# Attention and mixture of experts on one core: high and low parts of q and k made once and placed by transfers, token rows in pairs of d's, 256-column copies on VectorE

## The chip, the cores and the metric

The kernel runs on one core of a Trainium2 chip. The metric is the device time of one execution in microseconds (us). Three runs of the kernel before took 944.52, 946.16 and 946.60 us; the median, 946.16 us, is the time to which the change is compared.

## The reference

Attention with a decay bias over 64 heads (8 batches of 8), then a top-1 mixture of experts over the 4608 tokens, all in float32:

```python
scores = scale * np.matmul(q, k.transpose(0, 1, 3, 2))          # 8 x 8 x 576 x 576, head size 64
bias = -(cum[:, :, :, None] - cum[:, :, None, :])               # cum: running sum of max(s, 0)
scores = np.where(causal, -1e9, scores + np.minimum(bias, 0.0))
attn = softmax(scores)                                          # with 1e-9 added to the sum
x = (attn @ v) -> (B * S, H * D)                                # 4608 x 512
e_idx = argmax(x @ w_gate + modality_bias[modality_id])         # one of 8 experts a token
out[mask] = gate_w[mask, None] * (relu(x[mask] @ w1[e]) @ w2[e])
```

## The kernel before

**Stages.** The program first does attention for 32 pairs: a pair is one head of two batches (a = 0, 1), and eight pairs (the eight heads) make a group, which is 1152 finished tokens. After each group a routing step (`Route.group`) reads the tokens' gate values, finds each token's expert and slot, and nine indirect transfers issued by GpSimd (POOL, line 502) scatter the token rows into lists in HBM. After the attention the experts run over the lists (lines 657 to 886); their part of the program is not changed but for the order of the words in a token row.

**One pair.** A score is made in four steps. PE multiplies q by k twice into a PSUM tile `sp`: high parts (line 216: `QH` by `KA`, whose upper 64 rows are k's low part) and low parts with the bias rows (line 217: `QL` by `KB`). DVE adds the mask, copies the tile to `pe` in SBUF and finds the row's extreme (line 219). ACT takes the exponential (line 238). So it goes for nine tiles of a pair, in the order `ORDER`; the ninth, the rest of both batches, is `pep` (lines 230 to 238). Then `trans` turns each tile on PE (lines 248, 257) and copies it from PSUM into `PT`: on ACT (line 251), but for the numbers in `PTDVE`, which go to DVE (line 263). `tail` multiplies `V` by `PT` (lines 274, 279, into `o0` and `om`), copies the outcome to `oT` (ACT lines 283, 284; DVE line 287), multiplies by `pw` in two halves (lines 293, 296, into `ox`), and DVE scales and writes token rows `x` (lines 299, 301). `o0` and both halves share one PSUM buffer, `ox`.

**Operands.** q and k come from HBM in rows doubled on the host (`rawq`, `rawk`, 576 KB each a pair, line 152). `prep` rounds them to the matmul's format for the high parts and subtracts for the low ones: on POOL (lines 174, 192, 194), but for half of `QL`, which is on DVE (line 188) and reads what POOL has written. There are two sets of `QH`, `QL`, `KA`, `KB`; pair p+1's set is written while pair p runs. The bias rows of `KB` and `QL` come by transfers from HBM (lines 170, 171).

**The order.** The source interleaves the nine scores of a pair with the turning of tiles three steps behind (`LAG`), the tail of the pair before, the preparation of the next and the routing. The recording layer then sets one order for each engine from its own reckoning of when operands will be there. On the chip each engine works through its list in that order: an instruction whose operands are late holds everything behind it. SP issues the transfers in the same way.

Of the kernel before, what the change touches and what calls it, by code (L numbers as in the profile page):

```python
# [7 lines left out]
F32 = mybir.dt.float32  # L8
# [9 lines left out]
P = 128  # L18
KW = 576
XW = 72  # L20
# [7 lines left out]
PTDVE = (8,)  # L28


class Attn:
# [3 lines left out]
    def __init__(self, ctx, tc, qkv, s, ident, consts):  # L35
# [16 lines left out]
        self.mk = c.tile([P, 800], F32, name="mk")  # L52
        self.hold = [None]
        with tc.tile_pool(name="cst", bufs=1, side="right") as t1:
            sr = t1.tile([64, KW], F32, name="sr")
            nc.sync.dma_start(sr, s)
            raw = self.load_qk(0)
# [11 lines left out]
            self.raw = {0: raw}  # L69
            for _ in self.prep(0):  # L70
                pass
# [76 lines left out]
    def load_qk(self, pi):  # L148
        nc = self.nc
        raw = [self.ld.tile([P, 2, KW], F32, name="rawq"), self.ld.tile([P, 2, KW], F32, name="rawk")]  # L150
        for u in range(2):
            nc.sync.dma_start(raw[u], self.qkv[pi, :, 2 * KW * u:2 * KW * u + 2 * KW].rearrange("p (a k) -> p a k", a=2))
        return raw

    def load_v(self, pi):
        V = self.ld.tile([P, 2, 5, 64], F32, name="V", bufs=3)
        self.nc.sync.dma_start(V, self.qkv[pi, :, 4 * KW:].rearrange("p (a j d) -> p a j d", a=2, j=5))
        return V

    def load(self, pi):  # L160
        self.raw[pi] = self.load_qk(pi)
        self.V[pi] = self.load_v(pi)

    def prep(self, pi):
        nc = self.nc
        rq, rk = self.raw.pop(pi)
        QH, QL, KA, KB = (t[pi % 2] for t in (self.QH, self.QL, self.KA, self.KB))
        QHf, KAf = QH.bitcast(F32), KA.bitcast(F32)
        if pi:
            nc.sync.dma_start(KB.bitcast(F32)[64:74], self.ekd.rearrange("(a p) r k -> p r a k", a=2)[pi])  # L170
            nc.sync.dma_start(QL.bitcast(F32)[74:76, :, :KW], self.eqd.rearrange("(a p) r k -> p r a k", a=2)[pi])

        def high(o, i, e=None):
            (e or nc.gpsimd).tensor_scalar(o, i, 1.0, 1.0, ALU.mult, ALU.mult)  # L174

        lo, up = slice(0, 64), slice(64, P)
        for a in range(2):
            if pi:
                high(QH[:, a, :KW], rq[:, a])
            else:  # L180
                nc.scalar.copy(QH[:, a, :KW], rq[:, a])
        yield
        for a in range(2):
            high(KA[:, a], rk[:, a], nc.vector if pi == 0 and a == 0 else None)
        yield
        for a in range(2):
            if a == 0:
                nc.vector.tensor_tensor(QL[lo, a, :KW], rq[lo, a], QHf[lo, a, :KW], ALU.subtract)
            high(KB[lo, a], rk[lo, a], nc.vector if pi == 0 and a == 0 else None)
            yield  # L190
        for a in range(2):
            i = (nc.vector if pi == 0 and a == 0 else nc.gpsimd).tensor_tensor(KA[up, a], rk[up, a], KAf[up, a], ALU.subtract)  # L192
            yield
        (nc.vector if pi == 0 else nc.gpsimd).tensor_tensor(QL[lo, 1, :KW], rq[lo, 1], QHf[lo, 1, :KW], ALU.subtract)
        yield
# [7 lines left out]
    def score(self, st, i):  # L203
# [34 lines left out]
        nc.scalar.activation(t[:, :n], t[:, :n], AF.Exp, bias=m, scale=-1.0, accum_out=st["sums"][:, i:i + 1])  # L238
# [26 lines left out]
    def tail(self, st):  # L265
# [15 lines left out]
        nc.vector.tensor_scalar(rs, st["sums"], 1.0e-9, None, ALU.add)  # L281
# [7 lines left out]
        for g in range(2):  # L289
# [7 lines left out]
            src = xo[:, :4 * XW].rearrange("p (c a d) -> p a c d", c=2, a=2)  # L297
            rv = rs[:, 0:8].rearrange("p (a c) -> p a c", a=2)[:, :, 2 * g:2 * g + 2].unsqueeze(3).broadcast_to([P, 2, 2, XW])
            nc.vector.tensor_tensor(x[g][:, :, :, h].rearrange("p (a c) d -> p a c d", a=2), src, rv, ALU.mult)
            if g == 1:  # L300
                nc.vector.tensor_scalar(x[2][:, 0, :, h], xo[:, 4 * XW:5 * XW], rs[:, 8:9], None, ALU.mult)
            yield

    def run(self, npair, newx, done, setup):

        bg = []
        self.load(1)
# [669 lines left out]
```

## Time and profile before

| | us |
|---|---|
| median of three runs | 946.16 |
| profiled execution, its own time | 941.79 |
| its span, first to last instruction | 940.1 |
| busy in the span: PE / DVE / POOL / ACT | 860.9 / 633.8 / 576.1 / 527.5 |
| attention: first score, last write of a token row | 16.0, 465.3 |
| mean granted clock of PE, of full speed | 0.981 |

A profile of one execution stands behind these: each engine's instructions in time, what ended each wait, and the clock that PE was granted. Busy time is summed over stages with different limits, so the stage that the change touches is read by itself: the attention, about 16 to 465 us. A row of the grouped view gives line, engine, operation, tile, size, how often, then busy us, mean ns of one, the engine's idle us just before them and what ended most of it. A row of the timeline gives the start, the length, and in brackets the idle time before it and its releaser. A row of the stage table gives for each engine busy us and, behind x, its instructions, then the granted clock, the share of the DMA engines' time in use, and GB/s.

### The profile page before, as it was taken

The numbers are of one execution on the slowest core, as the hardware profiler recorded it, in microseconds if no ns is written. First come the engines' busy times: TensorE is split into PE (matmuls) and PEld (weight loads), VectorE is DVE, ScalarE is ACT, GpSimd is POOL, SyncE is SP. The second block draws the span as 40 slices with busy tenths as digits, with TensorE's granted clock in tenths as the row PEclk, the third lists the DMA queues.
The fourth block names the chain that finished last, engine by engine and source line by source line (L and its number), as shares of the span: only waits on it lengthen the run. The fifth ranks groups of instructions, "written<-read, shape, count | busy, mean of one in ns | idle before, by whom it ended". The sixth has DMA issues, their size and how long they took to land. (4 is left out here: it accounts for less than half of the span.)

```text
span 940.1 us, 16721 instructions
## 1 busy us (share of the span) xinstructions
PE 860.9 (92%) x5584; PEld 714.7 (76%) x5584; DVE 633.8 (67%) x1485; ACT 527.5 (56%) x1209; POOL 576.1 (61%) x478
## 2 busy tenths in 40 slices
PE   0799999799989998899988989999999999999984
PEld 0577777577667777677777979999999999999862
DVE  7477777577856778777556966566665566566771
ACT  3577776577656775587644525445544454454551
POOL 9576667666786766885064725556655465564760
PEclk9999999899999999999999999999999999999998
DMA  5743334533363335550577757666666666665940
GB/s 149 205 121 135 134 135 133 181 132 113 121 213 118 104 120 171 187 179 18 189 244 263 280 190 290 238 231 223 247 227 220 225 225 228 225 230 224 325 157 3
DMA packets 67564, 172.79 MB, mean 184 GB/s; under 512 B 12087, under 2 KB 12087, under 8 KB 67412
## 3 DMA queue, kind: packets, MB, share of 16 engines
q1 hardware_dynamic: 61620, 151.64, 47.1%
q0 software_dynamic: 5856, 20.06, 5.4%
q8 instruction: 45, 0.74, 0.3%
q14 instruction: 43, 0.35, 0.1%
HBM read 144.95 MB, written 26.80 MB: 183 GB/s over the span
## 5 line engine op out<-in xcount | busy, mean ns | idle before, releaser
L238 ACT ACTIVATE pe<-pe,mx 128x512 f32<-128x512 f32 (+3 forms) x256 | 143.8, 563 | 54.1 <-DVE mx L219 50.7
L279 PE MATMUL om<-PT,V 128*64 128x448 f32 (+3 forms) x640 | 124.9, 424 | 10.7 <-DVE PT L263 10.5
L791 ACT ACTIVATE hT<-hp 128x512 fp32r<-128x512 f32 x72 | 42.8, 595 | 156.9 <-PE hp L789 156.9
L251 ACT COPY PT<-pt 128x512 f32<-128x512 f32 (+3 forms) x256 | 106.7, 421 | 36.1 <-PE pt L248 28.9
L248 PE MATMUL pt<-ident,pe 128*128 128x128 f32 x640 | 121.9, 288 | 4.0 <-DVE PT L263 3.3
L219 DVE CUSTOM_DVE_ANT_0 pe<-sp,mk 128x512 f32<-128x512 f32 (+3 forms) x256 | 114.7, 478 | 12.9 <-PE sp L217 7.3
L775 POOL DMA_INDIRECT out<-ys,oi x36 | 37.3, 1037 | 133.5 <-DVE ys L774 50.5
L216 PE MATMUL sp<-KA,QH 128*128 128x256 f32 (+2 forms) x256 | 97.0, 386 | 20.1 <-DVE KA L192 16.0
L248 PEld LDWEIGHTS pt<-ident,pe 128*128 128x128 f32 x640 | 79.2, 146 | 40.5 <-issue 14.9
L174 POOL TENSOR_SCALAR QH<-rawq 128x576 fp32r<-128x576 f32 x62 | 47.0, 761 | 88.7 <-issue 80.9
L192 POOL TENSOR_TENSOR KA<-rawk,KA 64x576 fp32r<-64x576 f32 x63 | 95.9, 1541 | 2.6
L217 PE MATMUL sp<-KB,QL 76*128 76x256 f32 (+2 forms) x256 | 86.4, 343 | 7.3 <-DMA QL<-oh 7.3
L789 PE MATMUL hp<-xT,wcb 128*128 128x256 f32 x648 | 90.2, 283 | 1.6 <-DVE hT L792 1.6
L279 PEld LDWEIGHTS om<-PT,V 128*64 128x64 f32 x640 | 60.7, 136 | 40.6 <-DVE PT L263 14.9
L789 PEld LDWEIGHTS hp<-xT,wcb 128*128 128x128 f32 x648 | 83.6, 189 | 2.5 <-DVE hT L792 1.9
L792 DVE SCALAR_TENSOR_TENSOR hT<-hp,hT 128x512 fp32r<-128x512 f32 x72 | 49.2, 684 | 52.9 <-ACT hT L791 52.9
L789 PE MATMUL hp<-xT,wcc 128*128 128x256 f32 x528 | 76.4, 285 | 8.3 <-DVE hT L792 3.2
L768 PE MATMUL y<-wcb,hT 128*128 128x512 f32 x336 | 81.1, 398 | 0.0
L789 PE MATMUL hp<-xT,wca 128*128 128x256 f32 x552 | 78.1, 284 | 0.4 <-ACT xT L754 0.3
L789 PEld LDWEIGHTS hp<-xT,wcc 128*128 128x128 f32 x528 | 69.9, 194 | 9.3 <-DVE hT L792 3.4
L768 PEld LDWEIGHTS y<-wcb,hT 128*128 128x128 f32 x336 | 62.8, 188 | 14.8
L789 PEld LDWEIGHTS hp<-xT,wca 128*128 128x128 f32 x552 | 71.7, 190 | 1.3 <-ACT xT L754 0.5
(270 smaller groups left out, 1987.7 us busy)
## 6 DMA issues: line engine op xcount, KB each, us to landing
wrbw<-in_w SPq DMA_DIRECT2D x104, 512.0 KB
wraw<-in_w SPq DMA_DIRECT2D x56, 512.0 KB
rawq<-in_qkv SPq DMA_DIRECT2D x32, 576.0 KB
rawk<-in_qkv SPq DMA_DIRECT2D x32, 576.0 KB
xg<-lists SPq DMA_DIRECT2D x18, 576.0 KB
V<-in_qkv SPq DMA_DIRECT2D x32, 320.0 KB
lists<-z SPq DMA_DIRECT2D x8, 576.0 KB
ekd<-ek SPq DMA_DIRECT2D x1, 1440.0 KB
```

Of the source, the lines that this page charges most:

```text
L174: (e or nc.gpsimd).tensor_scalar(o, i, 1.0, 1.0, ALU.mult, ALU.mult)
L192: i = (nc.vector if pi == 0 and a == 0 else nc.gpsimd).tensor_tensor(KA[up, a], rk[up, a], KAf[up, a], ALU.subtract)
L216: nc.tensor.matmul(sp[:, :nn], QH[:, q0:q0 + P], KA[:, ab, :nn], start=True, stop=False)
L217: nc.tensor.matmul(sp[:, :nn], QL[:EXT, q0:q0 + P], KB[:EXT, ab, :nn], start=False, stop=True)
L219: ins = nc.vector.tensor_tensor_reduce(out=t[:, :n], in0=sp[:, :n], in1=self.mk[:, 512 - n:512], scale=-0.125, scalar=3.0e38, op0=ALU.add, ...
L238: nc.scalar.activation(t[:, :n], t[:, :n], AF.Exp, bias=m, scale=-1.0, accum_out=st["sums"][:, i:i + 1])
L248: nc.tensor.transpose(out=pt[:, P * j:P * j + P], in_=pe[:, P * j:P * j + P], identity=self.ident)
L251: cp(w[:, :, v:v + P], pt[:, :P * (c + 1)].rearrange("p (j q) -> p j q", q=P))
L279: nc.tensor.matmul(om[r, q0 - P:], V[:, ab, j, :], PT[ab][:, PTS * j + q0 if j < 4 else PTW - 64:PTS * j + KW if j < 4 else PTW], start=j ...
L768: self.last[0] = nc.tensor.matmul(y[u], hT[:, a, f, P * u:P * u + P], W[4 + f // 2][:, c, 512 * (f % 2):512 * (f % 2) + 512], start=f == 0 ...
L789: nc.tensor.matmul(hp[:, u], W[k][:, a, f:f + P], xT[:, c, k], start=k == 0 and i == 0, stop=k == 3 and i == 2)
L792: nc.vector.scalar_tensor_tensor(hT[:, 1, 2 * m:2 * m + 2], hp, 0.0, hs.bitcast(F32), ALU.max, ALU.subtract)
```

## The change

The host no longer doubles the rows: a pair's q (rows 0 to 63) and k (rows 64 to 127) come in one load `R` of 576 KB. `split` makes the high part `H` and the low part `L` of both at once, on POOL alone: two roundings and two subtractions of 128x576. `place` copies them into `QH`, `QL`, `KA` and `KB` by six transfers from SBUF to SBUF of 64 rows each (288 KB), and adds the two transfers of bias rows. `H` and `L` have one buffer each: the next `split` waits until the transfers have read them. `split` works two pairs ahead, `place` one pair ahead. Pair 0 is prepared as before, by `prep0`, from four loads of 64 rows.

Token rows hold d's in pairs (d pair, head, 2) where they held (d, head), so `x` is written in runs of two words; loads of `w1` and the reads of gate, token number and gate values follow. The sums of a pair are stored in the order in which `x` needs them. `PTDVE` takes tiles 1 and 5, the 128x256 copies, to DVE. The small sum in line 281 adds a tile of 1e-9 instead of a constant.

```diff
-PTDVE = (8,)
+PTDVE = (1, 5, 8)
...
+    def split(self, pi):
+        nc = self.nc
+        R = self.R.pop(pi)
+        H, L = (self.ld.tile([P, 2, KW], F32R, name=n, bufs=1) for n in ("H", "L"))
+        self.S[pi] = H, L
+        for a in range(2):
+            nc.gpsimd.tensor_scalar(H[:, a], R[:, a], 1.0, 1.0, ALU.mult, ALU.mult)
+            yield
+            nc.gpsimd.tensor_tensor(L[:, a], R[:, a], H[:, a].bitcast(F32), ALU.subtract)
+            yield
+
+    def place(self, pi):
+        nc = self.nc
+        H, L = (t.bitcast(F32) for t in self.S.pop(pi))
+        QH, QL, KA, KB = (t[pi % 2].bitcast(F32) for t in (self.QH, self.QL, self.KA, self.KB))
+        lo, up = slice(0, 64), slice(64, P)
+        nc.sync.dma_start(QH[lo, :, :KW], H[lo])
+        nc.sync.dma_start(QH[up, :, :KW], H[lo])
+        nc.sync.dma_start(KA[lo], H[up])
+        nc.sync.dma_start(KA[up], L[up])
+        nc.sync.dma_start(QL[lo, :, :KW], L[lo])
+        nc.sync.dma_start(KB[lo], H[up])
+        nc.sync.dma_start(KB[64:74], self.ekd.rearrange("(a p) r k -> p r a k", a=2)[pi])
+        nc.sync.dma_start(QL[74:76, :, :KW], self.eqd.rearrange("(a p) r k -> p r a k", a=2)[pi])
...
-        nc.scalar.activation(t[:, :n], t[:, :n], AF.Exp, bias=m, scale=-1.0, accum_out=st["sums"][:, i:i + 1])
+        o = 2 * (i % 4) + i // 4 if i < 8 else 8
+        nc.scalar.activation(t[:, :n], t[:, :n], AF.Exp, bias=m, scale=-1.0, accum_out=st["sums"][:, o:o + 1])
...
-        nc.vector.tensor_scalar(rs, st["sums"], 1.0e-9, None, ALU.add)
+        nc.vector.tensor_tensor(rs, st["sums"], self.eps, ALU.add)
...
-            src = xo[:, :4 * XW].rearrange("p (c a d) -> p a c d", c=2, a=2)
-            rv = rs[:, 0:8].rearrange("p (a c) -> p a c", a=2)[:, :, 2 * g:2 * g + 2].unsqueeze(3).broadcast_to([P, 2, 2, XW])
-            nc.vector.tensor_tensor(x[g][:, :, :, h].rearrange("p (a c) d -> p a c d", a=2), src, rv, ALU.mult)
+            src = xo[:, :4 * XW].rearrange("p (t d) -> p t d", t=4)
+            rv = rs[:, 4 * g:4 * g + 4].unsqueeze(2).broadcast_to([P, 4, XW])
+            nc.vector.tensor_tensor(x[g][:, :, :, h], src.rearrange("p t (d r) -> p t d r", r=2), rv.rearrange("p t (d r) -> p t d r", r=2), ALU.mult)
...
     def run(self, npair, newx, done, setup):
-        self.load(1)
+        self.load_r(1)
+        self.V[1] = self.load_v(1)
+        self.load_r(2)
+        for _ in self.split(1):
+            pass
...
-                    prepg = self.prep(pi + 1) if pi + 1 < npair else None
+                    if pi + 1 < npair:
+                        self.place(pi + 1)
+                    prepg = self.split(pi + 2) if pi + 2 < npair else None
                 self.score(sts[pi], i)
...
-                if k % 9 == 7 and pi + 2 < npair:
-                    self.load(pi + 2)
+                if k % 9 == 7:
+                    if pi + 3 < npair:
+                        self.load_r(pi + 3)
+                    if pi + 2 < npair:
+                        self.V[pi + 2] = self.load_v(pi + 2)
...
-    out = np.zeros((32, 128, 4 * KW + 640), np.float32)
+    out = np.zeros((32, 128, 2 * KW + 640), np.float32)
```

The source lines move by about 20 (line 216 of before is line 236 of the change, 219 is 239, 279 is 300, 299 is 320), and the recording layer sets another order, not only for the moved work.

On PE, before, from the last product of a pair (tile `sp_2211`) to the first product of `V` with its `PT`. The next pair reads the other set (`KA0`, `QH0`, `KB0`, `QL0`):

```order
L217 MATMUL sp_2211<-KB1_105,QL1_101 128x256
L216 MATMUL sp_2224<-KA0_102,QH0_98 128x512
L217 MATMUL sp_2224<-KB0_104,QL0_100 128x512
L216 MATMUL sp_2239<-KA0_102,QH0_98 128x512
L248 MATMUL pt_2216<-ident_61,pe_2156 128x128 x3
L217 MATMUL sp_2239<-KB0_104,QL0_100 128x512
L248 MATMUL pt_2233<-ident_61,pe_2175 128x128 x2
L216 MATMUL sp_2250<-KA0_102,QH0_98 128x384
L248 MATMUL pt_2246<-ident_61,pe_2187 128x128
L217 MATMUL sp_2250<-KB0_104,QL0_100 128x384
L216 MATMUL sp_2261<-KA0_102,QH0_98 128x256
L217 MATMUL sp_2261<-KB0_104,QL0_100 128x256
```

Four tiles of the next pair are finished here, both products, ahead of the products with `V` and of the tail. The same place in the changed kernel, the end of a pair's products with `V` and its tail, up to the next pair's tiles `sp_2078` and `sp_2092`; their first products (line 236) were made four rows above the first row shown:

```order
L300 MATMUL om_2119<-PT0_106,V_1679 64x448
L300 MATMUL om_2119<-PT2_108,V_1679 64x320
L300 MATMUL om_2119<-PT0_106,V_1679 64x320
L300 MATMUL om_2119<-PT2_108,V_1679 64x192
L300 MATMUL om_2119<-PT0_106,V_1679 64x192
L300 MATMUL om_2119<-PT2_108,V_1679 64x64
L300 MATMUL om_2119<-PT0_106,V_1679 64x64
L314 MATMUL ox_2160<-pw_111,oT0_109 128x144 x2
L314 MATMUL ox_2176<-pw_111,oT0_109 128x144 x2
L317 MATMUL ox_2176<-pw_111,oT0_109 128x72 x2
L237 MATMUL sp_2078<-KB1_105,QL1_101 128x512
L237 MATMUL sp_2092<-KB1_105,QL1_101 128x512
```

The second products of the next pair's first four tiles now stand behind the whole tail of the pair before. So it is listed at the end of pair 1 and of every pair from 4 to 30 (pairs are counted from 0), 28 times.

On DVE, before, the stretch that ends with the tail's first write of token rows (`x`); the masks are the next pair's:

```order
L219 ISA pe,mx<-sp,mk 128x384
L219 ISA mx 128x1
L219 ISA pe,mx<-sp,mk 128x256
L219 ISA mx 128x1
L281 TENSOR_SCALAR rs<-sums 128x9
L233 ISA pep,mx<-sp,mk 128x288
L233 ISA mx 128x1
L282 RECIPROCAL rs<-rs 128x9
L233 ISA pep,mx<-sp,mk,mx 128x288
L233 ISA mx 128x1
L287 COPY oT_109<-om 64x64 x2
L299 TENSOR_TENSOR x<-ox,rs 128x288
```

Five of the next pair's nine tiles are masked ahead of the first write. The same place in the changed kernel:

```order
L302 TENSOR_TENSOR rs<-sums,eps 128x9
L303 RECIPROCAL rs<-rs 128x9
L272 COPY PT_106<-pt 128x2x128
L308 COPY oT_110<-om 64x64 x2
L320 TENSOR_TENSOR x<-ox,rs 128x144x2 x2
L322 TENSOR_SCALAR xq<-ox,rs 128x36x2
L239 ISA pe,mx<-sp,mk 128x512
L239 ISA mx 128x1
L239 ISA pe,mx<-sp,mk 128x512
L239 ISA mx 128x1
L239 ISA pe,mx<-sp,mk 128x384
L239 ISA mx 128x1
```

The next pair's first mask comes behind both writes of `x` and that of `xq`. ACT's list follows: it has no exponential of the next pair ahead of the copies to `oT` (lines 304, 305).

The routing of a finished group moves too. Before, its DVE instructions stand singly between masks; in the changed kernel nine of them stand in one piece behind the last write of the group's last pair (`xq`), ahead of the next pair's first mask:

```order
L488 TENSOR_REDUCE lg<-x 128x32
L488 TENSOR_REDUCE lg<-xq 128x8
L490 TENSOR_TENSOR lg<-lg,mbs 128x72
L492 TENSOR_REDUCE rmx<-lg 128x9
L493 TENSOR_TENSOR lg<-lg,rmx 128x72
L497 SCALAR_TENSOR_TENSOR oh<-lg,ew 128x72
L498 TENSOR_REDUCE rmx<-oh 128x9
L500 TENSOR_TENSOR ohb_237<-oh,rmx 128x72
L522 TENSOR_REDUCE gs<-lg 128x9
L239 ISA pe,mx<-sp,mk 128x512
```

The next pair's masks, which stood between such instructions, now wait for all nine; the rest of the routing follows behind the masks.

More of the change, by code (lines that the diff above doesn't have):

```diff
@@ L68, in __init__ @@
             self.V = {0: self.load_v(0)}
-            self.raw = {0: raw}
-            for _ in self.prep(0):
-                pass
+            self.prep0(*raw)
+            self.R, self.S = {}, {}
     def exts(self, t1, cum):
```

91 lines of the change are left out of this document (41 added, 50 removed).

## The prediction

> **What bounds the kernel now.** I read the stage table first, then PE's idle time, then the timelines at the places where it stands idle.
>
> ```profile
> 49.90:99.90 50.00, 11.69 (x32) 6.04 (x32) 1.00 0.47 143
> 50.00:100.00 50.00, 49.58 (x342) 38.12 (x341) 35.87 (x135) 36.77 (x113) 34.23 (x37) 1.00 0.48 144
> 600.00:700.00 100.00, 100.00 (x662) 91.23 (x662) 60.91 (x56) 46.99 (x59) 56.12 (x26) 1.00 0.64 233
> ```
>
> The first row is the stage table for line 216 alone, which has eight products a pair: 32 in 50 us are four pairs, 12.5 us each. The second is the same stretch for all engines: PE is busy for 49.58 of 50 us, ACT and DVE for 37 and 36. In the undisturbed attention PE is the bound, because its order always has something ready. The third shows the experts' stage, PE busy throughout, on work that the change leaves alone. So the change decides the attention only, 16 to 465 us of the profile.
>
> Within the attention PE loses time at few places, above all here:
>
> ```profile
> PE om L279 <- DVE PT L263: 10.2, 8, 5.4
> 167.62 0.96 POOL L502 DMA_INDIRECT lists<-x,di  x1 [0.30 <-issue]
> 169.86 0.69 POOL L174 TENSOR_SCALAR QH<-rawq 128x576 fp32r<-128x576 f32 x1
> 170.59 1.21 DVE L188 TENSOR_TENSOR QL<-rawq,QH 64x576 fp32r<-64x576 f32 x1 [5.60 <-issue]
> 172.18 1.75 PE L279 MATMUL om<-PT,V 128*64 128x448 f32 x2 [5.38 <-DVE PT L263]
> 152.30:185.30 33.00, 6.36 (x17) 3.44 (x17) 0.90 0.49 168
> 264.00:294.50 30.50, 6.24 (x17) 3.30 (x17) 0.94 0.51 171
> 373.40:405.20 31.80, 6.24 (x16) 3.35 (x17) 0.95 0.57 188
> ```
>
> Read upward: PE waits 5.38 us for DVE's copy, which stands in DVE's list behind the subtraction of line 188; that waits for `QH` from POOL, and POOL is issuing scatters. It comes once a group. The last three rows are line 216 over two pairs each at these places: 33.0, 30.5 and 31.8 us instead of 25.0.
>
> **The change part by part.** *Preparation.* Line 188 leaves DVE, so this wait goes: 8.0 + 5.5 + 6.8, **-20 us**. POOL's ten operations a pair become four, the transfers take over the rest, and both work ahead. Is that cover enough?
>
> ```profile
> 18.00:25.20 7.20, 1.33 (x3) 0.83 (x3) 2.97 (x6) 0.00 (x0) 5.26 (x9) 1.00 1.00 205
> L174 POOL TENSOR_SCALAR QH<-rawq 128x576 fp32r<-128x576 f32 x62 | 47.0, 761 | 88.7 <-issue 80.9 <-PE sp L216 3.7 <-PE sp L217 3.6
> L194 POOL TENSOR_TENSOR QL<-rawq,QH 64x576 fp32r<-64x576 f32 x31 | 43.8, 1414 | 2.3
> ```
>
> In the first row the transfer engines are full (1.00) with one transfer out of 64 rows of SBUF (`ekd`), at 205 GB/s. Six placements of 295 KB at that rate take 8.6 us, and I add an estimated 1.5 us for issue and landing. They must end before the next `split` may write `H`; its first two roundings and the subtraction between them (0.76 + 1.41 + 0.76 = 2.9 us) must end before the next placement. That loop is 13.0 us a pair. It is hidden if a pair takes longer than 13.0 us; at 12.5 it would cost 0.5 us a pair. The Trainium skill, "SBUF — State Buffer", section "Door 1: The DMA port swizzle", says that a transfer's rate goes by the ports that its partitions reach, eight of sixteen for 64 rows, half of some 436 GB/s; the row agrees.
>
> *Order.* This decides. In the lists of the changed kernel a pair's first mask stands on DVE behind both writes of `x` and that of `xq` of the pair before, and the second products that it needs stand on PE behind the same tail. So at 28 boundaries (pair 1, pairs 4 to 30) nothing of the next pair's DVE or ACT work can run under the tail, whenever its operands come. One such end of a pair can be read in the profile of before: the last pair, which has no successor.
>
> ```profile
> 456.80 0.40 ACT L238 ACTIVATE pe<-pe,mx 128x128 f32<-128x128 f32 x1 [0.64 <-DVE mx L219]
> 457.44 1.44 ACT L251 COPY PT<-pt 128x384 f32<-128x384 f32 x4 [0.15 <-PE pt L248]
> 459.53 1.89 PE L279 MATMUL om<-PT,V 128*64 128x448 f32 x14
> ...
> 462.54 0.67 DVE L299 TENSOR_TENSOR x<-ox,rs 128x288 f32<-128x288 f32 x1
> 464.46 0.69 DVE L299 TENSOR_TENSOR x<-ox,rs 128x288 f32<-128x288 f32 x1 [1.25 <-PE ox L296]
> 464.99 0.32 DVE L301 TENSOR_SCALAR xq<-ox,rs 128x72 f32<-128x72 f32 x1
> ```
>
> From the end of the last exponential (457.20) to the end of `xq` (465.31) pass 8.1 us: copies, products with `V`, copies to `oT`, one half of `ox`, its write, the other half, its write. In the changed list the next pair's four first products stand among the products with `V`, and one 128x256 copy leaves ACT's row of four for DVE:
>
> ```profile
> 62.41 0.39 PE L216 MATMUL sp<-KA,QH 128*128 128x512 f32 x1
> 62.64 0.39 PE L217 MATMUL sp<-KB,QL 76*128 76x512 f32 x1
> L251 ACT COPY PT<-pt 128x256 f32<-128x256 f32 x64 | 23.5, 367 | 0.3 <-PE pt L248 0.3
> ```
>
> From start to start a 512-column product takes 0.23 us, so two of these, one of 384 and one of 256 columns make about +0.8; the copy -0.3 (0.37, less what DVE's hand-over costs). The end is 8.1 + 0.8 - 0.3 = **8.6 us**. The new pair begins only then: its first mask, then ACT's row of nine exponentials with three copies between (tiles of 512, 512 and 384 columns):
>
> ```profile
> L219 DVE CUSTOM_DVE_ANT_0 pe<-sp,mk 128x512 f32<-128x512 f32 x64 | 41.4, 677 | 5.8 <-PE sp L217 5.7
> L238 ACT ACTIVATE pe<-pe,mx 128x512 f32<-128x512 f32 x64 | 46.0, 723 | 13.2 <-DVE mx L219 13.2
> L238 ACT ACTIVATE pe<-pe,mx 128x384 f32<-128x384 f32 x64 | 39.6, 619 | 8.0 <-DVE mx L219 6.0 <-ACT PT L251 1.0 <-issue 0.7
> L238 ACT ACTIVATE pe<-pe,mx 128x256 f32<-128x256 f32 x64 | 32.9, 515 | 5.7 <-DVE mx L219 4.2 <-ACT PT L251 0.2
> L238 ACT ACTIVATE pe<-pe,mx 128x128 f32<-128x128 f32 x64 | 25.3, 396 | 27.2 <-DVE mx L219 27.2
> L238 ACT ACTIVATE pep<-pep,mx 128x576 f32<-128x576 f32 x32 | 24.9, 777 | 19.8 <-DVE mx L233 18.7 <-issue 1.2
> L251 ACT COPY PT<-pt 128x512 f32<-128x512 f32 x64 | 37.1, 581 | 8.7 <-PE pt L248 4.4 <-remote 1.7
> L251 ACT COPY PT<-pt 128x384 f32<-128x384 f32 x64 | 30.5, 477 | 26.3 <-PE pt L248 23.7 <-PE ox L296 0.7
> ```
>
> Two each of four sizes and one `pep`: 2 x (0.723 + 0.619 + 0.515 + 0.396) + 0.777 = 5.3 us; copies 2 x 0.581 + 0.477 = 1.6. The mask and its hand-over are 0.8. ACT's idle time for PE's turned tiles in such a row I bound by 0 and by one pair's share of the 384-column wait above (23.7 us in 64 copies, 0.74 a pair), and take 0.5. A pair is then 0.8 + 5.3 + 1.6 + 0.5 + 8.6 = **16.8 us**, against 12.5: 4.3 x 28 = **+120 us**. The bounds are 16.3 and 17.5, if hand-overs that the last pair did not show add up, +106 to +140. Placement (13.0) is hidden under it.
>
> *Copies and writes.* Tiles 1 and 5 on DVE are counted. The write of `x` in runs of two words has no row: above, the old write's 703 ns (below); below, a mask's, 453 ns for 288 columns. Two lie in the chain, so 0 to -0.5 us a pair. The reads and the place of the writes stay apart by 64 bytes, so I take the old row: **0** (0 to -14).
>
> ```profile
> L299 DVE TENSOR_TENSOR x<-ox,rs 128x288 f32<-128x288 f32 x64 | 45.0, 703 | 29.0 <-PE ox L296 20.2 <-PE ox L293 6.6 <-PE sp L217 1.1
> L233 DVE CUSTOM_DVE_ANT_0 pep<-sp,mk 128x288 f32<-128x288 f32 x32 | 14.5, 453 | 3.5 <-PE sp L231 3.3
> L468 DVE SCALAR_TENSOR_TENSOR oh<-lg,ew 128x72 f32<-128x72 f32 x4 | 4.5, 1125 | 0.0
> ```
>
> *Routing.* Nine instructions now hold a group's first mask: line 468 with 1.1 us and eight of 0.2 to 0.4, about 3.3 us, three times: +10. Before, they stood between masks at an unknown part of that; I take **+5** (0 to +10). The fourth group's routing lies behind the attention, as before.
>
> *Start.* Pair 1 needs its load, then `split`, then placement, one after another:
>
> ```profile
> 31.39 1.31 POOL L174 TENSOR_SCALAR KA<-rawk 128x576 fp32r<-128x576 f32 x2 [7.96 <-DMA rawk<-in_qkv]
> 35.73 0.48 PE L216 MATMUL sp<-KA,QH 128*128 128x512 f32 x1
> ```
>
> The load reaches POOL at 31.4, so pair 1 could start at 31.4 + 2.9 + 10.1 = 44 us instead of 35.7, while PE has pair 0's rest to do for most of it. **+6** (0 to +8).
>
> *Granted clock.* Where PE idles for part of a while its clock can halve.
>
> ```profile
> 256.41 0.41 PE L477 MATMUL ox<-ohb,tri 128*128 128x80 bf16 x10 [1.25 <-DVE ohb L471]
> 255.20:258.60 3.40, 2.19 (x24) 1.77 (x23) 3.10 (x15) 1.96 (x8) 0.86 (x1) 1.00 0.83 207
> 258.60:262.00 3.40, 3.40 (x16) 3.29 (x16) 1.73 (x6) 1.95 (x4) 1.79 (x2) 0.50 0.77 290
> 490.70:494.10 3.40, 1.56 (x11) 1.22 (x9) 1.53 (x1) 2.62 (x3) 3.40 (x2) 1.00 0.24 91
> ```
>
> After 3.4 us with PE busy for 2.19 the next 3.4 ran at 0.50; yet a stretch with only 1.56 busy was itself granted 1.00, so it is not certain. A new pair leaves PE idle for some 4.3 us in 16.8, in pieces of 0.5 to 1.3. One halved stretch costs up to 1.7 us of PE's work, not all of it on the chain: 0 to 1.2 a pair, 0 to +34. I take **+20**.
>
> The Trainium skill, "TensorE: Matmul & The Clock Gate", Part 1, has the clock fall after a whole idle window of about 3.4 us; by that none of these gaps would trip it and the term would be 0. The 2.19 row speaks against it.
>
> **Sum.** -20 + 120 + 0 + 5 + 6 + 20 = +131. On the profiled execution's own 941.8 that is 1073; the median of the three runs lies 4.4 above that execution, so **about 1078 us**.
>
> **The rivals.**
> - *The clock stays full*, the forecast without its 20: 1058 us. For it: the 1.56 row. Against it: the 2.19 row. 20%, and inside the range.
> - *The clock halves every pair and the waits add up* (17.5 and 1.2 more a pair, 18.7 us): 946 - 20 + 174 + 11 = 1111 us, up to 1125. 20%.
> - *Placement sets the pace* because the order costs less than I read: 13.0 us a pair, and scatters on POOL ahead of a `split` add up to 9 us a group: 946 + 14 - 20 + 11 + 0 to 27, 951 to 978 us. For it: one buffer of `H`. Against it: the lists put the tail in the chain whatever the placement does. 6%. By a page's 436 GB/s for SBUF to SBUF (the Trainium skill, "SBUF — State Buffer") this loop would be near 8.5 us and the rival void.
> - *Faster*: the next pair's work is late for another reason than its place in the list, so that PE keeps 12.5 us a pair and only the waits at line 188 go. Price: 946 - 20 + 6 = 932 us; it decides if a pair's end costs under 0.5 us more than now (28 x 0.5 = 14). The 49.58 of 50 busy speak for it, the 8.1 us of the last pair against. 4%.
> - *The change does not do what it says*, in that a transfer lands so late that placement adds to the chain instead of running under it: 16.8 + 2 to 4 us a pair, 1130 us and more. 6%.
>
> **How the numbers follow.** The forecast as it stands has 44%. 1030 at the low end takes in the clock at full and `x` at a mask's speed (1058 - 14, less 14 for hand-overs shorter than the last pair's), 1122 at the high end the halved clock; some 2 in 10 lie outside. Faster by over 0.2%: 4%; within 0.2%, about what a measurement of this kernel can tell from no change: 2%, the border between the placement case and the faster one; slower: 94%.
>
> **What would show it.** In the stage table the products of line 236 should come eight per 16 to 18.5 us from pair 5 on, PE busy for about 75% of the attention, the wait of DVE for POOL at line 188 gone. DVE's idle time before the first mask should stay small, with the writes of `x` just ahead of it, and ACT idle for 3 to 4 us ahead of each pair's first exponential. PE should wait at line 237 for nothing of SP. If it waits there for a transfer, placement was late and the rival on it is right; if pairs come at 12.5 us, the reading of the lists is wrong. The experts' stage should last as long as now.

## The result, and the profile after

| | before | changed |
|---|---|---|
| median, us | 945.39 (4 runs, 944.52 to 946.60) | 1085.49 (4 runs, 1079.31 to 1086.02) |
| profiled execution, its own time | 941.79 | 1086.02 |
| its span | 940.1 | 1084.3 |
| attention: first score, last write of a token row ends | 16.0, 465.3 | 16.7, 606.5 |
| mean granted clock of PE | 0.981 | 0.959 |

The changed kernel takes 1.147 times as long (95% interval 1.142 to 1.151), 140 us more; between the two profiled executions it is 144.2 us. All but 4 us of it lie in the attention.

The stage table of the changed kernel: the first row is line 236 alone (eight products a pair) over four pairs, the second all engines over six pairs from 208.6 us on, in the order PE, PEld, DVE, ACT, POOL, then clock, DMA share, GB/s.

```profile
234.70:303.20 68.50, 8.84 (x32) 5.73 (x32) 1.00 0.63 160
208.60:311.30 102.70, 82.83 (x506) 57.95 (x505) 48.02 (x201) 48.52 (x154) 24.42 (x24) 1.00 0.70 178
```

32 products in 68.5 us are 17.1 us a pair at full clock, where four pairs took 50 us before, and PE is busy for 81% of the time (about 75% had been expected) where it had 99%. No engine is full now. What each waits for shows in the end of one pair and the start of the next, in the timeline (chosen rows of DVE, PE and ACT, in order of time):

```profile
369.42 0.68 DVE L239 CUSTOM_DVE_ANT_0 pe<-sp,mk 128x512 f32<-128x512 f32 x1
...
376.23 1.01 DVE L284 COPY PT<-pt 128x256 f32<-128x256 f32 x4 [0.75 <-PE pt L278]
376.29 0.40 ACT L259 ACTIVATE pe<-pe,mx 128x128 f32<-128x128 f32 x1
376.71 0.97 PE L300 MATMUL om<-PT,V 128*64 128x448 f32 x2 [0.41 <-DVE PT L284]
377.61 0.77 PE L269 MATMUL pt<-ident,pe 128*128 128x128 f32 x5
378.73 0.50 PE L269 MATMUL pt<-ident,pe 128*128 128x128 f32 x2 [0.35 <-ACT PT L272]
379.09 0.44 ACT L272 COPY PT<-pt 128x128 f32<-128x128 f32 x2 [0.42 <-PE pt L269]
380.06 1.02 PE L236 MATMUL sp<-KA,QH 128*128 128x512 f32 x4
381.28 1.90 PE L300 MATMUL om<-PT,V 128*64 128x320 f32 x14
384.30 0.46 DVE L320 TENSOR_TENSOR x<-ox,rs 128x288 f32<-128x288 f32 x1
385.77 1.00 PE L237 MATMUL sp<-KB,QL 76*128 76x512 f32 x4
386.00 0.46 DVE L320 TENSOR_TENSOR x<-ox,rs 128x288 f32<-128x288 f32 x1 [1.25 <-PE ox L317]
386.38 0.28 DVE L322 TENSOR_SCALAR xq<-ox,rs 128x72 f32<-128x72 f32 x1
386.58 0.68 DVE L239 CUSTOM_DVE_ANT_0 pe<-sp,mk 128x512 f32<-128x512 f32 x1
387.36 0.72 ACT L259 ACTIVATE pe<-pe,mx 128x512 f32<-128x512 f32 x1 [3.67 <-DVE mx L239]
```

The first products of the next pair (line 236) are made at 380.06. Their second halves (line 237) come 5.7 us later, behind the tail, and wait for no transfer. The first mask follows `xq` at once, and ACT has been idle for 3.67 us when its first exponential starts. So it goes at the end of each pair from 4 on.

What the transfers do shows in the page's group of POOL's rounding (busy us, mean ns, then the idle time before it):

```profile
L176 POOL TENSOR_SCALAR H<-R 128x576 fp32r<-128x576 f32 x62 | 40.6, 674 | 283.6 <-DMA KB<-ekd 120.3
```

And in the view of waits, for SP (us in all, times, longest):

```profile
SPq L187 <- PE sp L236: 146.2, 22, 11.6
```

POOL stands idle for 283.6 us in all ahead of its roundings, and SP holds most placements back until PE is done with the set that they write. Preparation has time to spare here. It would be wrong to read POOL's long wait for a transfer as the cause: nobody waits for POOL.

### The profile page after: what moved, and what is told of

The parts are those of the page before. It is cut to its first block, busy times and chain, and to the rows that moved or that the text cites. A ratio compares the mean times of both kernels' runs of the same rounds, so it can differ in the third digit from the quotient of the medians.

```text
span 1084.3 us, 16771 instructions
## 1 busy us (share of the span) xinstructions
PE 923.8 (85%) x5584; PEld 738.4 (68%) x5584; DVE 600.0 (55%) x1519; ACT 501.6 (46%) x1145; POOL 437.6 (40%) x323
## 5 line engine op out<-in xcount | busy, mean ns | idle before, releaser
L176 POOL TENSOR_SCALAR H<-R 128x576 fp32r<-128x576 f32 x62 | 40.6, 674 | 283.6 <-DMA KB<-ekd 120.3
L269 PE MATMUL pt<-ident,pe 128*128 128x128 f32 x640 | 117.7, 302 | 26.3 <-ACT PT L272 25.5
L300 PE MATMUL om<-PT,V 128*64 128x448 f32 (+3 forms) x640 | 127.7, 430 | 13.7 <-DVE PT L284 13.7
L239 DVE CUSTOM_DVE_ANT_0 pe<-sp,mk 128x512 f32<-128x512 f32 (+3 forms) x256 | 111.6, 485 | 23.4 <-PE sp L237 22.6
L272 ACT COPY PT<-pt 128x512 f32<-128x512 f32 (+2 forms) x192 | 80.8, 435 | 62.6 <-PE pt L269 61.8
L308 DVE COPY oT<-om 64x64 f32<-64x64 f32 x64 | 14.2, 222 | 155.3 <-ACT oT L305 154.9
L236 PE MATMUL sp<-KA,QH 128*128 128x256 f32 (+2 forms) x256 | 77.6, 371 | 20.5 <-DVE frem L626 16.7
L178 POOL TENSOR_TENSOR L<-R,H 128x576 fp32r<-128x576 f32 x62 | 86.4, 1414 | 0.0
L236 PEld LDWEIGHTS sp<-KA,QH 128*128 128x128 f32 x256 | 49.2, 202 | 45.7 <-issue 16.9
L314 PE MATMUL ox<-pw,oT 128*128 128x144 f32 x256 | 57.4, 328 | 25.1 <-DVE x L320 18.4
L237 PE MATMUL sp<-KB,QL 76*128 76x256 f32 (+2 forms) x256 | 70.7, 350 | 7.9 <-DMA QL<-oh 6.5
```

What stands on the lines that cost most here:

```text
L178: nc.gpsimd.tensor_tensor(L[:, a], R[:, a], H[:, a].bitcast(F32), ALU.subtract)
L236: nc.tensor.matmul(sp[:, :nn], QH[:, q0:q0 + P], KA[:, ab, :nn], start=True, stop=False)
L237: nc.tensor.matmul(sp[:, :nn], QL[:EXT, q0:q0 + P], KB[:EXT, ab, :nn], start=False, stop=True)
L239: ins = nc.vector.tensor_tensor_reduce(out=t[:, :n], in0=sp[:, :n], in1=self.mk[:, 512 - n:512], scale=-0.125, scalar=3.0e38, op0=ALU.add, ...
L269: nc.tensor.transpose(out=pt[:, P * j:P * j + P], in_=pe[:, P * j:P * j + P], identity=self.ident)
L272: cp(w[:, :, v:v + P], pt[:, :P * (c + 1)].rearrange("p (j q) -> p j q", q=P))
```

## The experiments

**Masks first.** The changed kernel, all transfers kept; the tail is held in the lists of PE and DVE behind the next pair's tile that stands ahead of it in the source (`hold[0]` is that tile's mask, `mm` its last product).

```diff
-                if next(prev, 0) == 0:
-                    prev = None
+                with ExitStack() as after:
+                    if k < n:
+                        after.enter_context(self.tc.issue_after(self.hold[0]))
+                        after.enter_context(self.tc.issue_after(self.mm))
+                    end = next(prev, 0) == 0
+                if end:
+                    prev = None
```

> The changed kernel with one thing altered: the tail's instructions on PE and DVE are held in the lists behind the products and the mask of the next pair's tile that stands just before them in the source. All transfers stay. ORDER (the place of the tail in the lists made the pair 17.1 us): pairs come every 12.3 to 13.0 us, PE idle for less than 1 us a pair, time 935 to 965 us. PLACEMENT PACES (the loop of six transfers and the roundings takes longer than 12.5 us): 13.0 us a pair and more with POOL's scatters, 951 to 985 us, DVE or PE waiting for placed operands. LATE OPERANDS (the pair is long because the transfers land late): still 16 to 17 us, over 1040 us.

Measured: 941.33 us (10 runs, 936.25 to 948.35), 0.9965 times the kernel before (0.994 to 0.999). ORDER's time held; its pairs came a little shorter than expected. Line 236 over four pairs, and all engines there:

```profile
101.60:149.30 47.70, 11.28 (x33) 5.81 (x32) 1.00 0.86 216
101.60:149.30 47.70, 46.46 (x342) 36.38 (x342) 32.29 (x135) 34.26 (x106) 15.34 (x15) 1.00 0.86 216
```

11.9 us a pair here (the 33rd product is the next pair's first; 11.9 to 12.6 in most others between routings), PE busy for 97%. With one thing altered, 144 us of the changed kernel's time are gone: the order carries the whole loss, and no late operand does.

**Tail first alone.** The opposite: the kernel before, no transfer added. From pair 2 on, the second products and masks of the first three tiles of a pair are held behind the last product and the last write of the tail before.

```diff
+            if late:
+                yield
             nc.tensor.matmul(sp[:, :nn], QL[:EXT, q0:q0 + P], KB[:EXT, ab, :nn], start=False, stop=True)
...
+                if wait:
+                    for _ in prev:
+                        pass
+                    with self.tc.issue_after(self.last[0]), self.tc.issue_after(self.last[1]):
+                        for g in wait:
+                            next(g)
```

> The kernel before with its preparation by engines and without any added transfer; only the second products and masks of the next pair's first three tiles are held behind the last product and the last write of the tail. ORDER: 15.9 to 17.2 us a pair from pair 3 on, 1040 to 1085 us. LATE OPERANDS or PLACEMENT PACES: there are no placed operands here, so 12.5 us a pair and 946 us within 10.

Measured: 1062.45 us (4 runs), 1.126 times (1.123 to 1.128). Line 216 over four pairs:

```profile
80.70:147.00 66.30, 8.87 (x32) 5.90 (x32) 1.00 0.30 96
```

16.6 us a pair, with DMA share 0.30 and without one placed operand. Order alone makes 117 us, against 140 for the whole change. The expectation held.

**Preparation by engines.** The changed kernel with the preparation of before (`load_qk`, `prep` with line 188, doubled rows): the rest of the change alone, rows and copies (and the small sum with its tile of 1e-9).

```diff
-            raw = self.load0()
+            raw = self.load_qk(0)
...
-                    if pi + 1 < npair:
-                        self.place(pi + 1)
-                    prepg = self.split(pi + 2) if pi + 2 < npair else None
+                    prepg = self.prep(pi + 1) if pi + 1 < npair else None
```

> The changed kernel with the preparation of the kernel before (doubled rows, POOL and line 188, no placement), so the rest of the change alone: token rows in pairs of d's, tiles 1 and 5 turned by DVE. The lists have the masks ahead of the tail again. ORDER: 11.7 to 12.5 us a pair, the stalls of POOL's scatters are back, 925 to 950 us. COPIES AND ROWS COST (the loss comes from the work put on DVE): over 12.5 us a pair, 960 us and more.

Measured: 930.22 us (4 runs), 0.985 times (0.983 to 0.988), ahead of the kernel before and of the changed one; two runs further down come level with it (930.69 and 931.11). Four pairs of its line 218 (216 of before), then DVE's wait for POOL in the view of waits from 30 to 455 us:

```profile
74.30:123.20 48.90, 12.27 (x32) 6.18 (x32) 1.00 0.39 132
```

```profile
DVE QL L190 <- POOL QH L176: 15.8, 3, 5.6
```

12.2 us a pair, and the three waits for POOL (line 190 there is line 188 of before) are back, as ORDER expected.

**No placement.** The changed kernel, with the six transfers of `place` left out from pair 3 on.

```diff
+        if pi > 2:
+            return self.bias(pi, KB, QL)
         nc.sync.dma_start(QH[lo, :, :KW], H[lo])
```

> The changed kernel with the six placement transfers left out from pair 3 on (operands of pairs 1 and 2 are used again, so the output is not the reference's); loads, splits and the two transfers of bias rows stay, and the recording layer then lists the masks ahead of the tail by itself. ORDER: 11.7 to 12.5 us a pair, 920 to 945 us, about the same as with the order forced and all transfers, less 0 to 25 us for what the transfers still cost. LATE OPERANDS: the same time here, so this run by itself does not tell the two apart; against the run with the order forced it gives the price of the transfers.

Measured: 917.45 us (one run), 2.5 below the range. In its trace four or more masks of the next pair start ahead of the tail's first write of `x` at every end from pair 2 on, where the changed kernel has none from pair 3 on. No other edit was made: these transfers put the tail first. That they did it through the time that the recording layer reckons for them is argued, not shown. Beside the run with the masks first (941.33, transfers kept) the transfers cost some 24 us. Its pairs were no slower (11.9 us against 12.2 here); the loss lies at pair 3 (21.6 us against 13.7) and at the three routings (17.4, 17.6, 18.4 us against 13.2, 13.0, 13.0).

**Masks first, two more transfers.** The run with the masks first, both transfers into `QH` issued twice.

```diff
-        nc.sync.dma_start(QH[lo, :, :KW], H[lo])
-        nc.sync.dma_start(QH[up, :, :KW], H[lo])
+        for r in (lo, up, lo, up):
+            nc.sync.dma_start(QH[r, :, :KW], H[lo])
```

> The run with the masks first, and the two transfers into QH issued twice in each pair, so eight transfers of 64 rows instead of six; nothing else moves. LOOP IS THE PACE (in the run with the masks first a pair's 11.9 us are the loop of placement and rounding, which the 17.1 us of the changed kernel cover): the loop grows by two of eight transfers, 2.6 to 3.0 us, so 14.5 to 15 us a pair and 75 to 95 us on the whole, 1015 to 1035 us. PE IS THE BOUND (11.9 us are PE's work, and the loop has room left): under 1.5 us a pair, below 985 us.

Measured: 1051.79 us (one run). The loop of placement in the timeline, first of the run with the masks first, then of this one (POOL's rounding, and what it waited for); then four pairs of line 236 in this one, and what SP waited for at the repeated transfers (us in all, times, longest):

```profile
241.57 1.30 POOL L176 TENSOR_SCALAR H<-R 128x576 fp32r<-128x576 f32 x2 [7.77 <-DMA KB<-ekd]
242.90 0.62 SPq L187 DMA_DIRECT2D QH<-H  x1
253.43 0.67 POOL L176 TENSOR_SCALAR H<-R 128x576 fp32r<-128x576 f32 x1 [7.79 <-DMA KB<-ekd]
```

```profile
233.79 1.30 POOL L176 TENSOR_SCALAR H<-R 128x576 fp32r<-128x576 f32 x2 [12.24 <-DMA KB<-ekd]
248.75 1.30 POOL L176 TENSOR_SCALAR H<-R 128x576 fp32r<-128x576 f32 x2 [10.91 <-DMA KB<-ekd]
```

```profile
230.90:294.10 63.20, 10.79 (x32) 6.21 (x32) 0.87 0.89 219
```

```profile
SPq L188 <- DMA QH<-H: 80.9, 56, 4.9
```

From rounding to rounding it was 11.9 us, the same as the pair: with the masks first the loop and PE, 97% busy, are level. With two more transfers it is 15.0 us in the round shown, 3.1 more, about what LOOP IS THE PACE said, but 15.8, 15.3 and 16.5 us in the next three. The pairs took 15.8 us with it, and the time grew by 110 us, more than the 75 to 95 expected. So the loop has no room left there, as LOOP IS THE PACE says, though its price was off. That it, rather than PE, sets the 11.9 us is not shown: without the placement the pair was no shorter (12.2 us, the run before). The repeated transfers write the same rows as the first two and wait for them to land, so the 3.1 us are not the price of moving the bytes alone; what the lower clock of that stretch (0.87) adds was not tried apart. In the changed kernel's 17.1 us the loop of 11.9 was covered by 5 us.

**Copies alone, rows alone.** The kernel before with `PTDVE = (1, 5, 8)`; and with token rows in pairs of d's and the sums in the order of `x` (the small sum with its tile of 1e-9 came along).

```diff
-PTDVE = (8,)
+PTDVE = (1, 5, 8)
```

```diff
-            nc.vector.tensor_tensor(x[g][:, :, :, h].rearrange("p (a c) d -> p a c d", a=2), src, rv, ALU.mult)
+            nc.vector.tensor_tensor(x[g][:, :, :, h], src.rearrange("p t (d r) -> p t d r", r=2), rv.rearrange("p t (d r) -> p t d r", r=2), ALU.mult)
```

> The kernel before with tiles 1 and 5 turned by DVE, nothing else. COPIES GAIN (ACT's row of copies is what PE waits for in a pair): 12.2 us a pair instead of 12.5, 930 to 938 us, that is nearly all of the 15 us that the run with preparation by engines gained. PE BOUND (PE has always something ready, so a shorter row on ACT is worth nothing): 12.5 us a pair, 943 to 947 us.

> The kernel before with token rows in pairs of d's and the sums in the order of x, nothing else. ROWS HIDDEN (the write of x gets shorter, 0.46 us for 0.70, but the next pair's work covers it): 943 to 946 us. ROWS GAIN: two writes a pair with 0.25 us each less on the way of the next product into the same PSUM buffer, 31 x 0.25 to 0.5, 930 to 938 us.

Measured: 936.25 us (6 runs; 0.9915 times, 0.989 to 0.994) and 938.11 us (6 runs; 0.9937, 0.992 to 0.996). Line 216 of the first and line 218 of the second over four pairs (the 33rd product there is the next pair's), and the second's group of the write of `x` from 30 to 440 us:

```profile
74.40:124.20 49.80, 12.34 (x32) 6.21 (x32) 1.00 0.39 129
```

```profile
73.90:123.30 49.40, 11.86 (x33) 6.06 (x33) 1.00 0.36 124
```

```profile
L302 DVE TENSOR_TENSOR x<-ox,rs 128x288 f32<-128x288 f32 x60 | 27.4, 457 | 20.9 <-PE ox L299 15.2 <-PE ox L296 5.6
```

Each part gains, 7.5 and 5.7 us; together 13.2, where the run with both had 14.9. The copies' time is in the range of COPIES GAIN, but not for its reason: the pair is 12.45 us, hardly shorter, and the rest is at the pairs of the routing. The rows' time misses both ranges by a little; the write went from 0.70 to 0.46 us and the pair to 12.35.

**The wait at line 188 taken away.** The kernel before with this subtraction on POOL, and for balance one transfer in place of POOL's rounding into `KB`.

```diff
-                nc.vector.tensor_tensor(QL[lo, a, :KW], rq[lo, a], QHf[lo, a, :KW], ALU.subtract)
-            high(KB[lo, a], rk[lo, a], nc.vector if pi == 0 and a == 0 else None)
+                (nc.gpsimd if pi else nc.vector).tensor_tensor(QL[lo, a, :KW], rq[lo, a], QHf[lo, a, :KW], ALU.subtract)
+            if pi == 0:
+                high(KB[lo, a], rk[lo, a], nc.vector if a == 0 else None)
+            elif a == 0:
+                nc.sync.dma_start(KB.bitcast(F32)[lo], KA.bitcast(F32)[lo])
```

> The kernel before with line 188 on POOL from pair 1 on, and in return the rounding into KB replaced by one transfer of KA's lower 64 rows, so that POOL has about as much to do as before. STALL (the wait at line 188 behind POOL's scatters cost 20 us in three places): pairs 11, 19 and 26 come at 12.5 us, 924 to 932 us. CLOCK OR ROUTING (the places were long for the routing and the clock, and would be long without the wait too): 938 to 946 us.

Measured: 930.69 us (6 runs), 0.986 times (0.983 to 0.989), 13 us gained. Pairs 11, 19 and 26 took 12.5, 12.5 and 15.1 us where they had 19.8, 17.7 and 19.5, together 17 less; pair 3 lost 7 (19.2 us against 12.5). STALL holds.

**Together.** Three tries to add these gains: rows, copies and no wait at line 188 (the first); rows, no wait, and the set-up of the modality bias later (the second); the first with one rounding into `QH` on DVE and the later set-up (the third). A fourth left line 188 on DVE and relieved POOL by the transfer, with the later set-up. The rounding on DVE and the later set-up are these edits; the others are shown above.

```diff
-                high(QH[:, a, :KW], rq[:, a])
+                high(QH[:, a, :KW], rq[:, a], nc.vector if a else None)
...
-            setup = {3: lambda: A.setup(wg), 20: lambda: R.setup(mid, mb, A.wk.tile([P, KW], F32, name="pep", bufs=2))}
+            setup = {3: lambda: A.setup(wg), 38: lambda: R.setup(mid, mb, A.wk.tile([P, KW], F32, name="pep", bufs=2))}
```

> The rest of the change (rows, tiles 1 and 5 on DVE) with preparation by engines, line 188 on POOL and KB's lower rows by one transfer from KA. STALL: the 15 us of the rest and most of the 20 us of the wait add up, 12.0 to 12.2 us a pair, 912 to 925 us. POOL LATE (POOL, without DVE's help, falls behind at the scatters and PE waits for placed operands instead): 925 to 935 us, with PE waiting for QL or KB twice a group.

> The kernel before with token rows in pairs of d's, line 188 on POOL, KB's lower rows by one transfer, and the loads and sums of the modality bias at step 38 (pair 4) instead of step 20 (pair 2). ADDS UP: 13 us for the wait, 5 for the rows and some 4 for the set-up that stood in the way at pair 3: 918 to 924 us. DOESN'T ADD UP (PE's 12.2 to 12.5 us a pair are the floor whatever goes): 927 to 932 us.

> The run with the rest of the change and no wait at line 188, and in it the second rounding into QH on DVE (it reads a load only, so it waits for no other engine) and the set-up of the modality bias at step 38. POOL LATE was what that run lost (PE waited for KA and QL): with 0.76 us a pair taken off POOL the waits at pairs 11, 19 and 27 go, 12.2 us a pair, 918 to 926 us. If the waits come from somewhere else: 932 to 938 us as without it.

> The run with preparation by engines (930.2 us), with KB's lower rows by one transfer from KA in place of POOL's rounding, line 188 left on DVE, and the set-up of the modality bias at step 38. POOL LATE (in that run the wait at line 188 comes of POOL's load at the scatters, so 1.5 us a pair less on POOL shortens it): pairs 11, 19 and 27 come at 14 to 16 us instead of 17 to 19, 921 to 927 us. ORDER OF THE SCATTERS (POOL stands in its list behind the scatters whatever its load): 928 to 933 us.

Measured: 936.27 us (0.992 times, 0.989 to 0.995), 935.50 (0.992, 0.990 to 0.994), 931.11 (0.986, 0.985 to 0.988) and 934.24 (0.989, 0.987 to 0.991). None beats 930, and none reached the range that its expectation names first; the first two lie above both of their ranges, the third between its two. PE's waits for what POOL prepares, from 30 to 450 us, in the first and in the third:

```profile
PE sp L222 <- POOL QL L199: 2.9, 3, 1.0
PE sp L221 <- POOL KA L197: 1.7, 3, 0.6
```

```profile
PE sp L222 <- POOL QL L199: 2.6, 3, 1.0
PE sp L221 <- POOL KA L197: 0.7, 1, 0.7
```

So PE waited for POOL by 4.6 us in the first and by 3.3 in the third: POOL LATE is a small part of what that run lost. The third came out 5 us faster, but its relief and its later set-up were not tried apart: pair 3 went from 18.2 to 12.3 us, and pairs 11 and 27 still took 16.2 and 20.6. In the fourth DVE's wait at line 188 (190 there) is what it was with the rounding on POOL (15.8 us, three times); the view of waits from 30 to 455 us, then POOL's timeline at the second group:

```profile
DVE QL L190 <- POOL QH L176: 15.3, 3, 5.6
```

```profile
167.39 0.98 POOL L508 DMA_INDIRECT lists<-x,di  x1
173.73 0.96 POOL L508 DMA_INDIRECT lists<-xq,di  x1 [0.30 <-issue]
174.73 0.68 POOL L176 TENSOR_SCALAR QH<-rawq 128x576 fp32r<-128x576 f32 x1
```

Six scatters stand in one piece ahead of the rounding (the first and the last of them are shown), whatever POOL's load: by the wait it is ORDER OF THE SCATTERS, though the time lies 1.2 us above its range and pairs 11, 19 and 27 got no shorter (20.4, 17.7 and 20.2 us, where the run with preparation by engines had 19.1, 17.3 and 18.7). Why pair 18 took 18.9 us in the second, and pair 27 20.6 us in the third, stays open.

## Why the prediction was right

It said 1078 us; 1085.5 was measured. The step that decides, the order, stands by itself in both directions: taken out of the changed kernel it gives back 144 us, put into the kernel before it costs 117. Term by term, between the profiled executions (+144.2):

| term | forecast | measured |
|---|---|---|
| 28 ends of a pair in the chain | +120 (16.8 us a pair) | 17.15 us, against a mean of 12.6 before, over the 27 pairs from 4 on: +123 |
| waits at line 188 | -20 | gone; worth 17 by the run without them |
| routing ahead of the mask | +5 | 3 x 2.2 = +6.6 |
| start of pair 1 | +6 | 42.6 against 35.7 us: +6.9 |
| clock | +20 | about +21, an estimate |
| copies and write of `x` | 0 | 0.46 for 0.70 us, inside the chain's 17.15 |
| pairs 1 to 3 | none | 45.3 against 39.2 us: +6.2 |
| experts' stage | none | 477.8 against 474.8 us: +3, cause open |

The rows overlap: their sum is 150 for 144, and the halved clock in pairs 1 to 3 (10 us of it, some 5 us of time by the estimate below) stands in two of them. That the total came so close is in part luck: the two halves of the chain were off in opposite ways, and the clock's 20 was a choice within 0 to 34.

*The chain.* Its parts were off in opposite ways. From the first mask (369.42 us in that pair, 0.68 us long) to the end of the last exponential (376.69) it was 7.3 us, where 0.8 + 5.3 + 1.6 + 0.5 = 8.2 had been summed: ACT did not wait for PE there (0.5), and its instructions overlapped by some 0.4 in all. From the last exponential to the end of `xq` (386.66) it was 10.0 us for 8.6. In the last pair of before, from which that end was read, copies were done 1.7 us after the last exponential; here (378.73, 379.09) after 2.8. The same four tiles were left to turn in both. Chosen rows of the last pair of before:

```profile
455.49 1.01 DVE L263 COPY PT<-pt 128x256 f32<-128x256 f32 x4 [0.20 <-PE pt L257]
456.42 0.27 DVE L219 CUSTOM_DVE_ANT_0 pe<-sp,mk 128x128 f32<-128x128 f32 x1
456.86 0.77 PE L248 MATMUL pt<-ident,pe 128*128 128x128 f32 x5
```

There the last mask stood on DVE behind the four copies of line 263, so the last exponential itself was late (456.80, idle for 0.64 us before it), and PE turned the first of the four tiles before it had ended. Here the exponentials were through while DVE was still at these copies (line 284, 376.23 to 377.24), and PE, whose list has two products with `V` that need these copies (376.71) ahead of the four tiles, came to them 0.9 us after the last exponential (377.61). So the copies, which the end read from the last pair has at 1.7 us and the sum at 1.4, took 2.8: that is the mis-sized term. The next pair's four products took about 0.3 more than the 0.8 summed. The writes of `x`, taken at 0.70 and 0.46 us long, gave back some 0.4. The two ends of that bracket were right, the choice of the old row was not, nor its reason: the single words of before stand 32 bytes apart, the runs of two 64. The Trainium skill, "SBUF — State Buffer", section "Door 1: The DMA port swizzle", has a note that accesses run at full speed when at least two in a row hit the same line of 16 bytes; runs of two words are on the good side of that and single words are not, and the trace agrees (0.70 to 0.46 us, in the run with the rows alone too). The order in which the sources are read changed with the rows, and no run tells the two apart.

*Placement.* In the run with the masks first the 10.1 us from first issue to landing were 10.5 (242.90 to 253.43 above). The loop was 11.9 instead of 13.0 us, and not the 8.5 of the rival's last sentence, which divided by the rate for all partitions where these transfers have 64 rows: both roundings go ahead of the subtraction (1.30 instead of 2.9 us), as the first placements read `H` alone. That it is hidden was right, and from pair 2 on PE waited at line 237 for no placed operand. The rival on placement had its condition nearly right: once the order costs less, this loop is level with PE, but at 11.9 us, so 941 us came out and not 951 to 978.

*Routing.* The timeline of the third group, from `xq` to the next mask:

```profile
457.75 0.28 DVE L322 TENSOR_SCALAR xq<-ox,rs 128x72 f32<-128x72 f32 x1
457.94 0.41 DVE L488 TENSOR_REDUCE lg<-x 128x32 f32<-128x256 f32 x1
459.31 0.23 DVE L497 SCALAR_TENSOR_TENSOR oh<-lg,ew 128x72 f32<-128x72 f32 x1
460.13 0.68 DVE L239 CUSTOM_DVE_ANT_0 pe<-sp,mk 128x512 f32<-128x512 f32 x1
```

The mask comes 2.2 us later than the 457.94 of a common pair; the first group's comes as late. The 1.1 us taken for line 468 (497 now) was 0.23; more on that below.

*Clock.* Cut into stretches of 1 us, the attention of the changed kernel ran at or near half clock for 65 us, that of before for 19. The stage table at one such place, then in an undisturbed pair:

```profile
408.60:412.00 3.40, 2.19 (x9) 0.89 (x9) 1.73 (x7) 2.48 (x10) 0.00 (x0) 0.95 0.84 170
412.00:415.40 3.40, 3.26 (x12) 1.59 (x11) 0.42 (x1) 1.01 (x3) 0.00 (x0) 0.50 1.01 257
229.20:232.60 3.40, 2.39 (x12) 1.18 (x13) 1.73 (x7) 2.28 (x10) 0.31 (x1) 1.00 0.90 184
```

The two pairs there took 18.9 and 18.2 us, 2.8 more than two at 17.15, for some 6 us at half clock; 46 us more of it are about 21. Between the rivals (never, every pair) the truth was some pairs: stretches with 2.4 busy of 3.4 pass without a change. Cut into pieces of 3.4 us that end where the clock's spells begin, all eleven spells of this attention fell behind a piece with PE busy for 0.8 to 2.1 us; four pieces with 1.9 to 2.1 passed, none with less (from 43 us on). The rule of a whole idle window (the Trainium skill, "TensorE: Matmul & The Clock Gate", Part 1) fits none of the eleven.

*Missed.* Pair 3. SP's list has the set-up of the modality bias between two placements, and one of its small loads holds SP for 3.3 us. On DVE the set-up's instructions stand ahead of the copies that PE needs; PE waits 2.2 us for these, and DVE 0.65 us for the load:

```profile
67.34 3.33 SPq L464 DMA_DIRECT2D pep<-in_mb  x1
74.94 1.75 PE L300 MATMUL om<-PT,V 128*64 128x448 f32 x2 [2.21 <-DVE PT L284]
75.54 0.46 DVE L469 TENSOR_TENSOR mbs<-pep 128x288 f32<-128x288 f32 x1 [0.65 <-DMA pep<-in_mb]
```

The prediction looked at the queue only where pairs meet undisturbed, and had no term for this place. No run moves this set-up in the changed kernel. In the kernels with line 188 on POOL pair 3 took 19.2 and 18.2 us with the set-up at step 20 and 12.3 in both runs with it at step 38, so it fits as the cause. The rival *faster* fell: a pair's end costs 4.5 us more, not under 0.5.

## What to carry to other kernels

A scheduled kernel's order can hang on what its scheduler believes of operands; a transfer that is hidden on the chip can still move the list, and the list is paid for in each pair. Look at the lists at the boundary of two iterations first: what of the next one may run under the tail of this one. If nothing may, sum the tail in full; and if the order is wrong, pin it, as a few edges gave back 144 us here. POOL's or a queue's long wait says nothing until it is found who waits for it.

## What the runs showed of the hardware that was not expected

A DVE instruction on nine numbers a row can be held until POOL's instruction beside it ends. Line 281 (302 in the changed kernel) in the view by tile, as least, median and longest ns, of before and then of the changed kernel, where POOL is idle at most of these times:

```profile
L281 DVE TENSOR_SCALAR rs<-sums x32: 162/914/1039, 38.8 to 457.3; 128x9 f32<-128x9 f32 x32
```

```profile
L302 DVE TENSOR_TENSOR rs<-sums,eps x32: 149/152/970, 37.8 to 598.2; 128x9 f32<-128x9 f32 x32
```

In the kernel before 24 of the 32 last over 0.5 us, and each of these ends 0.03 us after the POOL instruction during which it started. So in the run with the rows, no wait and the later set-up, where one ends as POOL's first subtraction ends (two of 1.39 us from 264.94 on):

```profile
264.99 1.38 DVE L287 TENSOR_TENSOR rs<-sums,eps 128x9 f32<-128x9 f32 x1
264.94 2.77 POOL L197 TENSOR_TENSOR KA<-rawk,KA 64x576 fp32r<-64x576 f32 x2
```

The Trainium skill, "SBUF — State Buffer", section "SBUF: two separate sides", says that DVE and GpSimd share a pair of ports as an exclusive lock, held for a whole instruction; the 0.15 and 0.91 us agree. Line 468 shows the same: its 1.1 us is a mean of three of 1.43 us, each beside a subtraction of POOL, and one of 0.22 with POOL idle; in the changed kernel POOL is idle beside all four, and they take 0.23. Work that leaves POOL thus shortens DVE's small instructions, a gain that no term of the sum had.
